# Ranks of the list scheduler: a table in the source instead of a search at build time

## The chip, the cores and the metric

The kernel runs on one core of a Trainium2 chip. The metric is the device time of one execution in microseconds (us), median of three runs. TensorE (PE) multiplies, its weight loads (PEld) run beside it, VectorE (DVE), ScalarE (ACT) and GpSimd (POOL) work on tiles, and SyncE (SP) issues the DMAs. Each engine works through its own instruction list strictly in order and waits on semaphores of the others.

## The reference

Attention with capped scores, then two mixing blocks, all in 32-bit floats:

```python
scores = scale * np.matmul(q, k.transpose(0, 1, 3, 2))
scores = cap * np.tanh(scores / cap)
attn = np.exp(scores - np.max(scores, axis=-1, keepdims=True))
attn = attn / (np.sum(attn, axis=-1, keepdims=True) + 1e-09)
x = np.matmul(attn, v)                      # 4 batches, 12 heads, 448 rows, 64 wide
theta = x @ w_theta                         # x now 4 x 448 x 768
y = einsum(w_tok_r, x * cos(theta)) + einsum(w_tok_i, x * sin(theta))
u = x + y
x = u + np.maximum(u @ w_ch, 0.0)
h = np.maximum(x.T @ w_tok1, 0.0) @ w_tok2  # along the sequence, 256 wide
u = x + h.T
out = u + np.maximum(u @ w_ch1, 0.0) @ w_ch2  # 1536 wide
```

## The kernel before

The program is written as a recording: each call on an engine goes to `Plan.rec`, which makes an `Op` with its engine, its duration by a formula (`cost`), a rank (`prio`, the number of the call plus offsets such as -100 for weight loads) and its dependencies. At the end `Plan.emit` asks `Plan.plan` for an order of all 3872 Ops and writes the instructions out in that order; so every instruction of the trace has line L473.

`schedule` is a list scheduler: it keeps a clock, and whenever an engine is free it takes the ready Op of lowest rank, provided the rotating buffers that it needs (`SB`, `PS`: three `raw` tiles, two double PSUM tiles `pa`, four single ones `pm` and so on) are free and next in turn. Buffers of one tag are handed out in the order in which they were recorded. What was promised a buffer and can't have it goes to a list `waiting`, and comes back when one of that tag comes free. `schedule` also knows some habits of the chip as rules: a table load on ACT costs 1.3, a change of PE's tile form costs up to 0.19, a DMA lands 1.6 after its turn on one common queue plus `LATE`, and a DVE instruction whose operands all lie in SBUF takes up to 0.9 of its own duration longer while POOL is at work.

`plan` runs `schedule` 30 times; after each, `hurry` looks at PE's waits and lowers the rank of what came late. From the best of these `settle` tries 300 random changes of a few ranks near a wait and keeps those that don't lengthen the planned span.

What is computed, in the order of the recording: attention (`attn`) batch by batch in pairs of heads: scores into `pa` (named `sp`), tanh and exp on ACT (`t`, `tm`), products with V (`av`), row sums (`sm`, or in `av` for batches 2 and 3), then `finish`: DVE copies the product (`XT` or `xr`) and the sums (`sv`) out of PSUM, a DMA brings the sums into `pk`, DVE adds and inverts them, a DMA writes them to DRAM (`sr`), another brings them back spread over the partitions (`dn`), and DVE multiplies. For batch 0 `close` does this with two matmuls (`sel`, `spread`) instead. Beside attention the weights are converted (`convert`: a raw 64-bit tile `raw` becomes `cw`, then a high and a low part; DVE, ACT and POOL share the steps, and the result goes to DRAM and comes back as `w`, `WT`, `W`). Woven into batches 1 to 3 are the two mixing blocks of batches 0 and 1: `th` (theta), `rc` (its sine and cosine, on ACT and DVE), `tp` (transposes of `rc`), `zn` (their split into two parts), `tm` (mixing along the sequence), `wc`, `xp`/`xn`/`t`/`h` (the second block along the sequence), `c` (the wide products). PE has its last matmuls of attention shortly before 400 us; from 410 us on it runs the wide products of these two batches, and from 585 us on both mixing blocks of the other two.

The lines that matter for the change: the constants of the search (L80 to L86), `plan` with its helpers (L265 to L323), and the two places in `schedule` that take waiting Ops back (in `allocatable` and where a buffer comes free).

Of the kernel before, what the change touches and what calls it, by code (L numbers as in the profile page):

```python
# [5 lines left out]

# [158 lines left out]
class Plan:  # L165
# [111 lines left out]
    def settle(self, out):
        rng = random.Random(7)
        span, gaps, starts = self.span, self.gaps(out), [o.start for o in out]
        for _ in range(TRIES):  # L280
            at = rng.choices([g[0] for g in gaps], [g[1] for g in gaps])[0]
            near = [o for o in self.ops if at - 14.0 < o.start < at + 1.0]
            some = rng.sample(near, min(len(near), rng.choice((1, 2, 4, 8))))
            old = [(o, o.prio) for o in some]
            for o in some:
                o.prio += rng.uniform(-30.0, 12.0)
            new = self.schedule()
            if self.span < span + 1e-6:
                span, out, gaps = self.span, new, self.gaps(new)
            else:  # L290
                for o, x in old:
                    o.prio = x
                for o, x in zip(out, starts):
                    o.start = x
            starts = [o.start for o in out]
# [2 lines left out]
    def gaps(self, out):
        end, found = 0.0, []
        for o in out:  # L300
            if o.eng == "PE":
                if o.start - end > 0.05:
                    found.append((o.start, o.start - end))
                end = max(end, o.start + o.dur)
        return found

    def hurry(self, out):
        ops, end, late = self.ops, 0.0, set()
        for o in out:
            if o.eng != "PE":  # L310
                continue
            if o.start - end > 0.3 and o.deps:
                x, n = o, 0
                while x.deps and n < HOPS:
                    d = max((ops[i] for i in x.deps), key=lambda y: y.wait)
                    if d.wait < end - 12.0:
                        break
                    if d.start > d.ready + 0.2:
                        late.add(d.n)
                    x, n = d, n + 1  # L320
            end = max(end, o.start + o.dur)
        for n in late:
            ops[n].prio -= PUSH  # L323
# [1290 lines left out]
```

## Time and profile before

| | |
|---|---|
| median of 3 runs | 939.85 us (937.0 to 941.76) |
| the profiled execution | 940.55 us |
| its span, first to last instruction | 938.8 us |
| granted TensorE clock, mean | 0.996 |
| PE busy | 916.3 us |
| PEld busy | 715.5 us |
| DVE, ACT, POOL busy | 614.9, 464.5, 286.5 us |
| instructions | 13346 |

The profile is of one execution. A busy time is the union of an engine's instructions; a wait of PE shorter than the tail of the matmul before it doesn't show as idle. "Idle before" with an engine behind an arrow names what ended the wait. PEclk is the share of full TensorE speed that was granted. The names of tiles are the program's, without buffer numbers. The profiled execution is 0.7 us longer than the median, and 1.75 us longer than its own span.

### The profile page before, as it was taken

How to read it: one execution, taken by the hardware profiler on the slowest of the kernel's cores; microseconds unless marked ns; L12 is line 12 of the kernel's file. 1: busy time of each engine (PE TensorE's matmuls, PEld its weight loads, DVE VectorE, ACT ScalarE, POOL GpSimd, SP SyncE). 2: the span in 40 equal slices, each digit the busy share in tenths (PEclk: the TensorE clock that was granted, in tenths of full speed). 3: DMA queues.
4: the chain of work that ended last, by engine and by line, in shares of the span. 5: the costliest groups of instructions: out<-in, count | busy, mean ns of one | idle time of the engine just before them, and what ended most of it. 6: DMA issues, size and time to landing. Idle time of an engine off the chain costs nothing.

```text
span 938.8 us, 13346 instructions
## 1 busy us (share of the span) xinstructions
PE 916.3 (98%) x4875; PEld 715.5 (76%) x4875; DVE 614.9 (65%) x1022; ACT 464.5 (49%) x743; POOL 286.5 (31%) x231
## 2 busy tenths in 40 slices
PE   8898999999999989999999999999999999999998
PEld 2222665656666667789999999999899999999997
DVE  7997879787795565756656584444794678445342
ACT  6787887977975646524354360424531254021010
POOL 3554334352243222103223261111641264311000
PEclk9999999999999999999999999999999999999999
DMA  6777756575547853246868769811213114443232
GB/s 211 258 251 259 227 170 210 186 265 171 174 126 229 277 150 116 88 138 215 279 206 259 224 225 296 319 35 68 84 40 132 48 55 123 128 159 100 90 127 92
DMA packets 80090, 159.80 MB, mean 170 GB/s; under 512 B 10264, under 2 KB 60312, under 8 KB 80024
## 3 DMA queue, kind: packets, MB, share of 16 engines
q1 hardware_dynamic: 80024, 158.95, 52.6%
q8 instruction: 38, 0.62, 0.3%
q14 instruction: 28, 0.23, 0.1%
HBM read 111.61 MB, written 47.18 MB: 169 GB/s over the span
## 4 chain that ended last, share of the span: by engine, by line
PE 78%; ACT 4%; DMA 3%; DVE 3%; POOL 1%; issue 1%; SPq 0%; ACTq 0%; POOLq 0%
PE c L473 29%; PE P L473 10%; PE th L473 8%; PE tm L473 7%; PE t L473 7%; PE wc L473 6%; PE av L473 5%; PE sp L473 3%; PE tp L473 2%; PE xp L473 1%; DMA raw<-wu 1%; ACT t L473 1%; DMA pk<-sv 1%; DMA dn<-sr 1%; POOL cw L473 1%
## 5 line engine op out<-in xcount | busy, mean ns | idle before, releaser
L473 PE MATMUL c<-g,w 128*128 128x448 f32 x816 | 166.6, 364 | 0.0
L473 POOL TENSOR_TENSOR cw<-cw,raw 128x384 uint32<-128x384 uint32 (+2 forms) x94 | 97.8, 1042 | 219.9 <-DVE cw L473 172.4
L473 PEld LDWEIGHTS c<-g,w 128*128 128x128 f32 x816 | 153.0, 187 | 12.1
L473 PE MATMUL tm<-WT,zn 128*128 128x448 f32 x483 | 108.2, 372 | 0.0
L473 PE MATMUL c<-XHL,w 128*128 128x448 f32 x522 | 107.8, 366 | 0.0
L473 PEld LDWEIGHTS c<-XHL,w 128*128 128x128 f32 x522 | 97.8, 188 | 8.7
L473 PEld LDWEIGHTS tm<-WT,zn 128*128 128x128 f32 x483 | 88.3, 188 | 13.2 <-ACT zn L473 2.1
L473 PE MATMUL th<-XHL,w 128*128 128x448 f32 x432 | 97.6, 372 | 0.0
L473 DVE TENSOR_TENSOR XT<-c,XT 128x448 f32<-128x448 f32 x68 | 42.3, 623 | 80.3 <-PE c L473 80.2
L473 PEld LDWEIGHTS th<-XHL,w 128*128 128x128 f32 x432 | 79.1, 188 | 14.3 <-issue 5.9
L473 ACT ACTIVATE t<-sp,consts 128x896 f32<-128x896 f32 x72 | 72.2, 1004 | 30.1 <-PE av L473 10.9
L473 ACT ACTIVATE t<-t,consts 128x896 f32<-128x896 f32 x72 | 74.8, 1044 | 1.8
L473 POOL TENSOR_TENSOR t<-t,t 128x896 f32<-128x896 f32 x24 | 53.4, 2227 | 64.7 <-PE av L473 30.6
L473 POOL TENSOR_TENSOR XHL<-XT,XHL 128x448 fp32r<-128x448 f32 x36 | 47.8, 1338 | 74.9 <-ACT XHL L473 49.3
L473 PE MATMUL av<-t,vt 128*64 128x448 f32 x288 | 66.5, 565 | 3.1 <-ACT t L473 2.9
L473 PE MATMUL wc<-XHL,w 128*128 128x448 f32 x306 | 67.1, 373 | 0.0
L473 DVE SCALAR_TENSOR_TENSOR cw<-raw,cw 128x384 uint32<-128x384 uint32 (+2 forms) x94 | 64.7, 688 | 2.5
L473 PEld LDWEIGHTS wc<-XHL,w 128*128 128x128 f32 x306 | 57.2, 190 | 11.8 <-issue 7.0
L473 ACT CAST w<-cw 128x384 fp32r<-128x384 f32 x72 | 34.6, 508 | 36.2 <-PE c L473 17.7
L473 DVE TENSOR_TENSOR w<-cw,w 128x384 fp32r<-128x384 f32 x72 | 49.6, 706 | 3.3 <-ACT w L473 2.6
L473 PE MATMUL sp<-kq 64*128 64x448 f32 (+1 forms) x240 | 47.2, 576 | 2.8 <-ACT t L473 2.7
L473 PEld LDWEIGHTS av<-t,vt 128*64 128x64 f32 x288 | 16.3, 137 | 41.8 <-issue 20.7
(171 smaller groups left out, 1453.6 us busy)
## 6 DMA issues: line engine op xcount, KB each, us to landing
w<-cu SPq DMA_DIRECT2D x47, 768.0 KB
raw<-wu SPq DMA_DIRECT2D x72, 384.0 KB
cu<-w SPq DMA_DIRECT2D x72, 384.0 KB
kq<-kqd SPq DMA_DIRECT2D x24, 448.0 KB
vt<-vd SPq DMA_DIRECT2D x24, 224.0 KB
f<-cw SPq DMA_DIRECT2D x28, 192.0 KB
F<-f SPq DMA_DIRECT2D x28, 192.0 KB
out<-XT SPq DMA_DIRECT2D x24, 224.0 KB
```

The lines of the kernel that those rows point to most:

```text
L473: getattr(eng[o.eng], name)(*map(real, a), **{x: real(y) for x, y in k.items()})
```

## The change

The search at build time (`settle`, `gaps`, `hurry` and the loop in `plan`) is taken out. Instead a string of 77 lines holds 3872 whole numbers, compressed; Op number n gets the rank n + 0.5 times its number, which takes the place of the recorded rank with its offsets too. `schedule` then runs once. The numbers were worked out beforehand by a longer search of the same kind. In `schedule` itself one thing is different: when a buffer comes free, only those waiting Ops come back that hold the next buffer in turn (`wake`), where before all that waited for the tag came back to be tried again.

```diff
-ROUNDS = 30
-TRIES = 300
-HOPS = 6
-PUSH = 15.0
+RANKS = r"""
+c-kG92V9or_r`BPG-vK|{M1UV{#t38X64F}WontLVOmydWtlTantLxaH<`E>BBkQM#TErIL>z!1h)9Tn!27<>^PKblzI^xq56^qw=RW7Ut}|}Tyu#=qF?V
...
+"""
     def plan(self):
-        best = None
-        first = {o.n: o.prio for o in self.ops}
-        for _ in range(ROUNDS):
-            out = self.schedule()
-            if best is None or self.span < best[0]:
-                best = self.span, {o.n: o.prio for o in self.ops}
-            self.hurry(out)
-        for o in self.ops:
-            o.prio = best[1][o.n]
-        return self.settle(self.schedule())
...
+        shift = np.frombuffer(zlib.decompress(base64.b85decode("".join(RANKS.split()))), "<i2")
+        for o, x in zip(self.ops, shift, strict=True):
+            o.prio = o.n + 0.5 * x
         return self.schedule()
...
-                for n in waiting.pop(tag, ()):
-                    heapq.heappush(ready[ops[n].eng], (ops[n].prio, n))
+                wake(tag)
             return None
+
+        def wake(tag):
+            want = self.order[tag][nxt[tag]] if nxt[tag] < len(self.order[tag]) else None
+            some = [n for n in waiting.get(tag, ()) if any(b is want for b in ops[n].bufs)]
+            for n in some:
+                waiting[tag].remove(n)
+                heapq.heappush(ready[ops[n].eng], (ops[n].prio, n))
...
-                        for n in waiting.pop(b.tag, ()):
-                            heapq.heappush(ready[ops[n].eng], (ops[n].prio, n))
+                        wake(b.tag)
```

The 3872 Ops, their dependencies and the buffers are the same in both programs; the number of instructions differs only in waits and in ACT's table loads (22 before, 20 now). Within their engine's list half of PE's Ops move by two places or more, the furthest by 28. A change of tile form comes 325 times on PE before and 320 times now. The order at three places:

**PE and DVE in batch 1, where `finish` waits for its DMA (135 to 145 us of the trace).** DVE, before: the sums of one head are inverted (`RECIPROCAL pk`), and four rows later another product is multiplied by its `dn`.

```order
L473 SCALAR_TENSOR_TENSOR pk_1189<-pk_1189,consts 56x16
L473 RECIPROCAL pk_1189<-pk_1189 56x16
L473 TENSOR_TENSOR zn_1283<-tp_1264,zn_1277 128x384
L473 TENSOR_SCALAR cw_1319<-cw_1319 128x384
L473 SCALAR_TENSOR_TENSOR cw_1319<-raw_1151,cw_1319 128x384
L473 TENSOR_TENSOR XT<-XT,dn_1280 128x448
L473 CAST XHL<-XT 128x448
```

DVE, now:

```order
L500 SCALAR_TENSOR_TENSOR pk_1187<-pk_1187,consts 56x16
L500 RECIPROCAL pk_1187<-pk_1187 56x16
L500 TENSOR_SCALAR cw_1310<-cw_1310 128x384
L500 SCALAR_TENSOR_TENSOR cw_1310<-raw_1216,cw_1310 128x384
L500 TENSOR_TENSOR XT<-XT,dn_1239 128x448
L500 CAST XHL<-XT 128x448
L500 TENSOR_TENSOR XT<-tm_1101,XT 128x448
```

Now the multiplication that stands there is that of the head before, whose `dn` is issued on SP ahead of the `pk` load that the first row needs; before, SP issued that `dn` behind it. The head that stood there before is multiplied 13 rows further down, behind the transposes shown next. PE, before (two groups of transposes of one `rc`):

```order
L473 MATMUL th_1315<-XHL,w_953 128x448 x6
L473 MATMUL tp_1372<-ident,rc_1110 128x128 x4
L473 MATMUL sp_1380<-kq_975 128x448 x2
L473 MATMUL tp_1396<-ident,rc_1110 128x128 x3
L473 MATMUL av_1239<-tm_1254,vt_992 64x448
L473 MATMUL av_1404<-tm_1254,vt_1174 64x448
```

PE, now:

```order
L500 MATMUL th_1334<-XHL,w_940 128x448 x3
L500 MATMUL tp_1355<-ident,rc_1107 128x128 x4
L500 MATMUL th_1334<-XHL,w_940 128x448 x12
L500 MATMUL tp_1385<-ident,rc_1107 128x128 x3
L500 MATMUL av_1184<-tm_1236,vt_963 64x448
L500 MATMUL av_1394<-tm_1236,vt_1110 64x448
```

Between the two groups of transposes stood two score matmuls, and now stand twelve matmuls of theta.

**DVE in batch 3, where a product leaves PSUM (340 to 350 us).** `COPY xr` empties the PSUM tile that PE's next scores (`sp`) need; `cw` are steps of `convert`. Before:

```order
L473 SCALAR_TENSOR_TENSOR h_551_3252<-t_550_3192,h_551_3252 128x512
L473 COPY sv_3290<-av_3046 128x448
L473 TENSOR_TENSOR XT<-t_559_3263,XT 128x448
L473 TENSOR_SCALAR cw_3248<-cw_3248 128x384
L473 SCALAR_TENSOR_TENSOR cw_3248<-raw_3134,cw_3248 128x384
L473 COPY xr_3305<-av_3046 128x448
L473 TENSOR_TENSOR XT<-t_560_3279,XT 128x448
```

DVE, now:

```order
L500 TENSOR_TENSOR w_3216<-cw_2887,w_3216 128x384
L500 TENSOR_TENSOR xn_3244<-xp_3219,xn_3232 112x4x128
L500 TENSOR_TENSOR xn_3244<-xp_3210,xn_3232 112x4x128
L500 TENSOR_SCALAR cw_3242<-cw_3242 128x384
L500 COPY xr_3263<-av_3063 128x448
L500 SCALAR_TENSOR_TENSOR cw_3242<-raw_2925,cw_3242 128x384
L500 TENSOR_TENSOR t_3098<-t_3098,t_3164 128x896
```

Before, the copy stood four rows behind that of the sums and behind two steps of `convert`. Now it stands 13 rows behind that of the sums, but PE has moved the other way: between the last `av` matmul that writes this tile and the scores that need it there were a pair of `av`, three `t` and three `wc` matmuls, and now there are six `av`, 24 `t` of 256 columns and 12 `t` of 448 columns.

**DVE in the mixing of batches 2 and 3 (615 to 620 us).** `zn` is read by PE's next `tm` group; `rc<-th` are the first two steps on a new theta. Before:

```order
L473 TENSOR_TENSOR rc_5642<-rc_5642,XT 128x448
L473 TENSOR_TENSOR XT<-tm_5570,XT 128x448
L473 TENSOR_TENSOR XT<-tm_5596,XT 128x448
L473 TENSOR_TENSOR zn_5687<-tp_5614,zn_5622 128x512
L473 TENSOR_SCALAR rc_5699<-th_5648 128x448
L473 SCALAR_TENSOR_TENSOR rc_5699<-th_5648,rc_5699 128x448
L473 TENSOR_TENSOR zn_5687<-tm_5596,zn_5622 128x384
```

DVE, now:

```order
L500 TENSOR_TENSOR zn_5571<-th_5487,zn_5557 128x384
L500 TENSOR_TENSOR rc_5619<-rc_5619,XT 128x448
L500 TENSOR_SCALAR rc_5681<-th_5641 128x448
L500 TENSOR_TENSOR XT<-tm_5565,XT 128x448
L500 TENSOR_TENSOR XT<-tm_5581,XT 128x448
L500 SCALAR_TENSOR_TENSOR rc_5681<-th_5641,rc_5681 128x448
L500 TENSOR_TENSOR zn_5701<-tp_5614,zn_5624 128x512
L500 TENSOR_TENSOR zn_5701<-tm_5581,zn_5624 128x384
```

The first row of the two `rc<-th` now stands ahead of two additions to `XT`, the second directly ahead of `zn`; before, `zn` came first. On PE six `tm` matmuls and ten transposes stand between the theta matmuls that these rows need and the `tm` group that needs `zn`.

Elsewhere, in the attention of batch 1 (80 to 90 us), PE had three `av` pairs in a row, the sums, and then three score groups in a row; now `av` and `sp` alternate.

## Rows read from the trace of the kernel before

**Rows 1.** The page: busy time by engine, and one costly group.

```profile
PE 916.3 (98%) x4875; PEld 715.5 (76%) x4875; DVE 614.9 (65%) x1022; ACT 464.5 (49%) x743; POOL 286.5 (31%) x231
...
L473 POOL TENSOR_TENSOR t<-t,t 128x896 f32<-128x896 f32 x24 | 53.4, 2227 | 64.7 <-PE av L473 30.6
```

**Rows 2.** Busy time by stretch; columns in its first line, clock and DMA as shares.

```profile
core 0: us, PE busy (x) PEld busy (x) DVE busy (x) ACT busy (x) POOL busy (x), PEclk, DMA share, GB/s
0.00:78.00 78.00, 71.66 (x386) 19.79 (x390) 70.30 (x137) 57.84 (x69) 38.85 (x33) 1.00 0.76 256
78.00:92.00 14.00, 11.14 (x64) 3.04 (x58) 9.29 (x19) 10.15 (x13) 5.21 (x5) 1.00 0.57 174
...
125.00:150.00 25.00, 23.05 (x119) 13.31 (x118) 19.79 (x35) 19.50 (x32) 9.26 (x7) 0.93 0.70 217
...
275.00:300.00 25.00, 23.37 (x124) 16.99 (x123) 18.52 (x38) 14.85 (x30) 10.23 (x9) 1.00 0.72 211
...
343.00:353.00 10.00, 7.63 (x33) 4.44 (x30) 6.62 (x8) 2.96 (x4) 3.11 (x2) 0.83 0.57 150
...
399.00:404.00 5.00, 4.44 (x31) 3.75 (x30) 2.98 (x5) 2.02 (x3) 0.00 (x0) 1.00 0.56 130
...
680.00:938.80 258.80, 255.22 (x1340) 236.18 (x1338) 143.24 (x212) 58.81 (x112) 59.57 (x50) 1.00 0.31 99
```

**Rows 3.** Timeline of PE, 78 to 92 us: start, us, work, idle before.

```profile
80.98 0.97 PE L473 MATMUL av<-t,vt 128*64 128x448 f32 x4 [0.56 <-ACT t L473]
82.95 0.97 PE L473 MATMUL av<-t,vt 128*64 128x448 f32 x4 [1.00 <-ACT t L473]
...
89.58 1.94 PE L473 MATMUL sp<-kq 64*64 64x448 f32 x12 [0.95 <-ACT t L473]
```

**Rows 4.** The chain that ended last, 125 to 149 us: start, us, what.

```profile
131.77 7.28 DMA dn<-sr
...
144.00 0.90 PE tp L473 x3
```

**Rows 5.** Busy time by stretch behind two waits; clock is the third number from the end.

```profile
144.00:146.00 2.00, 2.00 (x11) 0.81 (x11) 1.97 (x4) 1.09 (x3) 0.00 (x0) 0.50 1.02 357
146.00:148.00 2.00, 2.00 (x12) 0.45 (x12) 1.54 (x5) 1.95 (x4) 0.00 (x0) 0.67 0.94 317
...
349.00:351.00 2.00, 2.00 (x6) 0.58 (x3) 0.94 (x2) 0.44 (x1) 0.00 (x0) 0.50 0.76 113
351.00:353.00 2.00, 2.00 (x9) 1.80 (x8) 0.00 (x0) 1.97 (x3) 0.00 (x0) 0.72 0.78 299
```

**Rows 6.** Timeline of all engines, 342 to 351 us.

```profile
344.31 2.10 POOL L473 TENSOR_TENSOR t<-t,t 128x896 f32<-128x896 f32 x1 [1.85 <-PE av L473]
344.35 2.28 DVE L473 TENSOR_SCALAR cw<-cw 128x384 uint32<-128x384 uint32 x1
...
347.14 0.62 DVE L473 COPY xr<-av 128x448 f32<-128x448 f32 x1
...
347.90 0.86 PE L473 MATMUL sp<-hl 64*128 64x448 f32 x6 [2.37 <-DVE xr L473]
```

**Rows 7.** Timeline of DVE, 615 to 620 us.

```profile
617.49 0.68 DVE L473 TENSOR_TENSOR zn<-tp,zn 128x512 fp32r<-128x512 f32 x1
618.17 0.62 DVE L473 TENSOR_SCALAR rc<-th 128x448 int32<-128x448 f32 x1
```

**Rows 8.** Timeline of PE in the same stretch.

```profile
615.52 1.38 PE L473 MATMUL tm<-WT,zn 128*128 128x448 f32 x6
...
618.30 0.60 PE L473 MATMUL tp<-ident,rc 128*128 128x128 f32 x4
618.65 1.68 PE L473 MATMUL tm<-WT,zn 128*128 128x448 f32 x7
```

**Rows 9.** Timeline of DVE, 408 to 421 us.

```profile
409.89 0.24 DVE L473 RECIPROCAL pk<-pk 56x16 f32<-56x16 f32 x1
...
420.15 0.63 DVE L473 TENSOR_TENSOR xr<-xr,dn 128x448 f32<-128x448 f32 x1 [1.70 <-DMA dn<-sr]
```

More of the change, by code (lines that the diff above doesn't have):

```diff
@@ L1 @@
+import base64
 import heapq
-import random
 import math
 import re
+import zlib
 from contextlib import ExitStack, contextmanager
@@ L92 @@
 PAT2 = (1, 0, 0, 1, 0, 0, 0)
+RANKS = r"""
+c-kG92V9or_r`BPG-vK|{M1UV{#t38X64F}WontLVOmydWtlTantLxaH<`E>BBkQM#TErIL>z!1h)9Tn!27<>^PKblzI^xq56^qw=RW7Ut}|}Tyu#=qF?V
+B*Uk;0Fc=_^`=(z9y?UkH)G4T5Q)Io^@qFN=4xwJC2_~N3JUv5@UZhN~^@``KIVykDBTu#5)`cAi)?MXdz)ANI3{bD|hEIGUGe$>7ESV=hjZ-
+<<_53akub+5PQII(s$^I7VU|AMnC$S|vmw6-
+#>;dUq4=@{P$7uLD!c<Pt6^AuVU&N`prxsK0n`BD1W>zvsdVIOif%L4Z&a!mG>z30yJv7Fx}P&dkR5`pEI%B!q3vc;L;_LY3uC%;=G?1S=HE9()R;G{TjN
+|rOxPVzgchjplKbhgPy=CIYpd2*wde?y%kr7~NRt4)-
+Z@|_HHp4g9_9rg@QCDT;`<TH(RW?8H4D^`kq(lg1VSd*+D@M)9%oHW&QI#!oSZwa(#d!p=i);pd$PDSgw-NonLHTA4g;~C=2^eneiJQ<$(POfLR&+nQlSI
@@ new lines @@
+kgtEJN%J_bq#*9cQnx=UJVcPzfoiUtHV%Rc6T{Yl7X*DY75gW%fuX)3wIA;_-
+EooM}#!oobJfxt^AC&*|aBdivI!;uLx|y6W1e?8o+BmEW~TOILe}{e=~6f37{MSMk)aXW9Ao{>K$6k8`%#U9A7<eUEW{@0woYzGs-
+z+J45gc$n%Ob7tCMl5L-I{H%kn8Lk++zms7Fm-
+ct6+HLz3m1VfQSlddRvNok7%i8KD=c=7#b+uaA{VHs7HMNFWfu&OF?>T0@ZwGi1tOVQF`QBOV+;;bM=UQLM30dkcbTzhqk;bl-rA5V)CBJNGNlDQwPkwkZ
+P-d5Y?&|)?%-iYlSOuQ7PKB~J-
+BoRuYkFCjXNFeLF8YIt=MDE!tD#fJ`qQ=2J<49_X>HfBJ6Qca8?1As<4XHlN8BG;bv^YwStXN8p0>A?Y$$%NB(SW1NonbUJ+~iiay!;==ZL23TJ5Nz`ixn
+vr^_N;9bE5QuX<K%h)mKUI!EgmV@l;a-CEMi<y%(ha;#X_q_WOg#qK6gW|w{A=_O&BA-_tL4AJkf6d^10mX5^YWOd9Nra;WR0e1Y80_zRWOOh?~^=&gsYn
@@ new lines @@
+s}o^V^r*8j&u4$-X14gE^7_e-KF-qG!uO8p@vXm{}@YoaJq=Iv(euZbTpIadnkE3-ujsT;HLy#RUw*-REOU*gH_A%qK>|VRx-
+7c*~Uo=h$)7@c7Q_)Ip(c=+o%U6dO~ZOO6DWD&1C=IDESrB8EdDhp84$bGq>?E5>6lLLi~F`1w4nndH9%sHnwRbiaG)sizH7ivN#2+xA4Q)Jk2Tj*x74sA
+>$rto})0k0Z(_4UqR(Dtp<Z5WNfikHM#s=q_2T$h9;q@*N7{MD5E*;4q0^yJP+#*Im6CD+MFnI&~Of1CBx53VvE-
+H<`UUE4^JY=!4+s_m!1Uq)8OlCzBEC+bAh;zse+2b^$(DAQ0O`Q3ucO_iPA0**HKV>pWP2M&PkJ($)i>pCZjcr49N$PN#w~e?LgMd;p|G}L=eoUYAf?6HR
+*4C8!R`VhY0Pa4RskfZp5F8rir-
+*Lq%YB87~7lJ5#%&v)}M{15x!wQHG5BL<{6Ctk1@yC=hB&9FgS4b8zl&{v`w4`Z@0csD%fpk2%r{+%k2BY{j#o#C#W39@TorTLZGlvxemSCf>C*?aXP;_(
@@ new lines @@
+<-8Bl=2anGDhzDEL#}MH5|fQ=iW-$$I|UhL7J<NgA*+hDmJ%YDtvcME5y2=@gJX3!@2~vmJXgs077S-WW7;iRmnam_tD!7aN<gnFUw*Al;4Z-
+l?yn&HCuzH>yKV6!kIKdi8vb$<vo!a-N)CkG&7ze<v87#g_M;(S$0wlxXXjfby)l4;SmSqj?K_g3)vc(Rg5g8Q$cOw<lo#C<q<o=NN2mqt=Zg-
+>aF~Sbl(~NANrZn=`53t++jSSM4A-3(4MOvg$as-
+f+LWi!U`yEz^m)^D($~fM3IG_9FiN&C^(Xf68p2mbD=>EKYg_Mk_EKEkV7z@wqMjKSX)guy~dHkAThDoS&uM3YP?~^;usA3WMoR1GF)>jl+0;njPufEUI$
+1-
+a#$h3nFJ=;)ygNFW<p(7+?3P6bD%Uy!nmDikKL^chf8^W^%?CXw+a&m>(?e(%U(|GTeND`fAHu&O8Oi+wda}`_tu9ZUS?ino@)NQnbus$0D@$BdYNBlSuu
@@ new lines @@
+C{G86-rFgmtZ1<qqsd7u|$v}NyrlaI!Ch90SZ_MvW?CMA)Mc%um{H%?nBlBK&vTF$_jAQy8r+-
+Sj@|#Tr6OoI!4in{U{T9!<ps5$|_@P*we+l%$VIxZ}q3DiaGmg`4$tTiGduV_4!}C3G|B^W@8FEVMn#uIn=4OB{HQS{g*!HKE%$GcOknLDu)(Ldh7=4a(#
+xuvf3I8*s6rB2NkW<Zm;)!>EX&rKM?P@Ysrb<m>zTxFYQ=~|4N(&8>Z28$t)!oh<n93pU!#V^nJJVmUz(fhv`Bk&VFu8GyZvaOVVY4!~{av6vge<Q?1@qn
+zl2F(v)0j`*VGg~f{mcTe4M!FI`MZ{R-3&%;--
+2`j87{C|s)OjtS#X*S2j2hc?B{6{6I3!MHD%hGr^983^pWP$z<8%(?|tP<{7mHYr<h4DP)m2<^Ad8T2K6+TzPy6GtWSSzNe&#L6FnfJt-
+OgRTa(F_id5F?)X_QcdmEMgp>w1*Sig<3(qxyMrso|1r{nln&3wwuJ)HUBYB?(LSo;?(UxL%t#(Pt_tzKU}<x|1$%r?<v#WzfZk>DK0&wXfgKJOpmV-io*
@@ new lines @@
+$@&0J-N0>WJXPM9-DGPHmUEd?9-
++i|wCufMU6Xz~h@2aNo_<AnYk5v*df=`iy@|+}_ULmQ_xIso(}0@sF|{EOKTGH)dtmQl*cp%3;=w!^&oat+Nny|XRJDQFNTd@?m3VnqE5KR<>P0J13kM%&
+b<-b@4SC#!-K$}(2DKuYK2`^fHv!cp=zThwyBKe;a!;sBl-
+~aV2B5<$U>YN>^eN4huGm{b#W_WnDj*A|P;<|qp{w9`k9*i2n7K)n8OC=b^9OY(p6C*_r>Si6;d?E0_ZEA5qK7`5_AYVVA$Rv-
+>nQ$QFaIxSHYe0$%E%|WpWyF3ko$soH)&JU;hj~!;uBx9g4#We>i@F&1T_t3-
+9_xI;f(WS;)nF7&0uka>8lDH&j8aO==O6oUJj^34{B>hi1&ZSbG0RYPr<t+PD`e{d8fhwu(<*>Lzz8JX^t$G9^4%6OQ9Ttp~0wg3L1zfeivQl1GuSTwvvw
+t@)NzKfOFs0hS~;io4|U8__3=1Ej<Cj4e-
@@ L95, in regroup @@
+5QBW0qv<d~#NOKQbJ*^2)MsQ+icq&hR%Id2}q#|r!&uilF5&u7<V7E$J6bshTY2M&X%XCq+j1bWWa8{&_@U!&QfRIDX>TpF=!CjE9S@h#VX#ak2qL)&-
+ob0_RG&oJLzE>}?~evL*Amr?i`>Zf;Np9&sVz{4<)gyQ*rGHt!yl`*iBL!CZS&i*aba)DiIVd6DB-a)Q(<@-
+20Ccwsxa;^0v&*ITZqUK2eI`GcG{ZQR<?0ipF1o2lb{IsMk(S8n(G3<^Z|FW3_6ZHQ9X5!<8
+"""
 def regroup(shape, pattern, sizes):
@@ L265, in plan @@
     def plan(self):
-        best = None
-        first = {o.n: o.prio for o in self.ops}
-        for _ in range(ROUNDS):
-            out = self.schedule()
-            if best is None or self.span < best[0]:
-                best = self.span, {o.n: o.prio for o in self.ops}
-            self.hurry(out)
-        for o in self.ops:
-            o.prio = best[1][o.n]
-        return self.settle(self.schedule())
[L277 to L295, printed above, removed]
-        return self.schedule()
@@ L298, in gaps @@
[L298 to L323, printed above, removed]
+        shift = np.frombuffer(zlib.decompress(base64.b85decode("".join(RANKS.split()))), "<i2")
```

36 lines of the change are left out of this document (added).

## The prediction

> **What bounds the kernel now.** I read the page first: PE is busy 916.3 of 938.8 us of span [rows 1], so its waits that show make 22.5 us, and no reordering can give back more than these and what the clock loses behind them. Then I asked where they lie, with the table of stretches [rows 2]: 6.34 us in the first 78 us (78 less 71.66), 2.86 from 78 to 92, 1.95 from 125 to 150, 1.63 from 275 to 300, 2.37 from 343 to 353, 0.56 from 399 to 404, and 3.58 behind 680 us, most of it the tail after the last matmul, which no rank can shorten. What these stretches leave of the 22.5 us, 3.2, is spread out. The clock column adds a loss that isn't idle time: 0.93 over 25 us is 1.75 us, 0.83 over 10 us is 1.7 us. So the floor for any order is near 940.55 - (22.5 - 3.6) - 3.45 = 918.2 us, and the question is how much of 22 us the table gets. Behind 404 us PE waits little; the change is decided in the first 404 us, and there by single places.
>
> **The change, part by part.** Work: nothing is added or removed, since the Ops are the same; the changes of tile form on PE are 325 before and 320 now, and two table loads less on ACT lie beside PE's work. I cost both at nothing. The `wake` rule brings back the one Op that can get its buffer instead of all; those others would have gone back to the list, so it costs nothing either, unless a form or table preference chose among them. What is left are places.
>
> *Attention, 0 to 92 us.* Before, PE did three `av` pairs in a row and waited for ACT's exponentials ahead of the second and third, 0.56 and 1.00 us, and then three score groups in a row, with 0.95 us ahead of the next [rows 3]. Now `av` and `sp` alternate, so ACT gets scores while PE does products. ACT was busy 10.15 us of these 14 and PE 11.14 [rows 2]; fully overlapped, 11.1 would do. Since two steps of ACT follow each other for each score group, I take 2.0 of the 2.86 us as gone (bounds 0 and 2.86). In the first 78 us ACT is at work 57.84 us and DVE 70.30, the order on PE is much the same, and part of the 6.34 us is the first load. I take 1.5 (bounds -1 and 3).
>
> *125 to 150 us.* The chain of waits shows DVE held by a DMA, `dn<-sr`, for 7.28 us until 139.05, a row of late DVE work behind it, and PE's transposes at 144.00 at the end [rows 4]. PE idles 1.95 us, and then runs at a granted clock of 0.50 from 144 to 146 and 0.67 from 146 to 148, that is at the lower of its two levels, 1.2 GHz, for more than 3 us [rows 5]; this loses 2 x 0.50 + 2 x 0.33 = 1.66 us. The place costs 3.6 us. Now the multiplication that stood there has its DMA wait 13 rows later, the one in its place has a DMA that SP issues before one that DVE needs anyway, and PE has twelve theta matmuls between the two transposes instead of two score matmuls. I take all 3.6 as gone (bounds 0 and 3.6).
>
> *275 to 300 us.* Of 1.63 us, one score group more ahead of the product that waited takes 0.86, the length of such a group at 347.90 [rows 6]: 0.8 (bounds 0 and 1.6).
>
> *343 to 353 us.* DVE's copy of `xr` comes at 347.14, behind a step of `convert` that took 2.28 us beside an addition of POOL of 2.10; PE waits 2.37 us for it [rows 6], and then has a clock of 0.50 and 0.72 in the two stretches from 349 to 353 [rows 5], a loss of 2 x 0.50 + 2 x 0.28 = 1.56. Together 3.9 us. Now some 40 matmuls stand between the last product in that tile and the scores that reuse it, instead of eight. All 3.9 gone (bounds 0 and 3.9).
>
> *399 to 404 us.* Between transposes and the matmuls that read them stood one group; now there are three small groups and one of sums. 0.5 of 0.56.
>
> Gone: 2.0 + 1.5 + 3.6 + 0.8 + 3.9 + 0.5 = 12.3 us.
>
> *Added, near 616 us.* `zn` now stands behind both `rc<-th` steps and two additions. From the end of theta: four DVE steps of about 0.62 and `zn` with 0.68 [rows 7], 3.2 us, and 0.2 for the handing over. PE has meanwhile six `tm` matmuls, at most 1.38, and ten transposes, at 0.09 each by the 0.35 us from the start of four to the next group [rows 8], together 2.2 us. PE waits some 1.2 us where it didn't (bounds 0 and 1.6); I take 1.3, with the transposes' own wait for `rc`.
>
> *Places that I can't see.* Two of the largest waits before came of what the planner doesn't know: the DMA took 7.28 us, and the step of `convert` is booked with 0.16 + 0.00052 x 384 = 0.36 us and at most 0.9 times that on top, 0.68, but took 2.28. The new order was fitted to the same planner and will meet such things at other places. The price of a place where they reach PE is 3.6 to 3.9; the old order had two in full. I take one, 3.8 us (bounds none and three, 0 to 11.4), since the slack at the known places has grown.
>
> A rule of the skill bears on this. The row shows that the DVE step ended at 346.63, just after POOL's addition at 346.41 [rows 6]. The Trainium skill says, in "SBUF — State Buffer", section "SBUF: two separate sides", that VectorE and GpSimd share one pair of ports as an exclusive lock, and that the loser blocks for the whole instruction; the row agrees. By this rule each of POOL's 24 additions of that shape, 2227 ns on average [rows 1], can hold a DVE step up to 1.6 us longer than the planner thinks, in either order alike, and the closer the table follows the planner, the less it leaves for that. This speaks against the change, and is the reason for the second case below, whose time comes from the rows.
>
> **Sum.** 12.3 gone less 1.3 and 3.8 leaves 7.2 us: 940.55 - 7.2 = 933.35 for an execution like the profiled one, which lies 0.7 above the median; so 932.6, rounded **932.5 us**.
>
> **The rivals.** A measurement can tell about 0.5% here, 4.7 us: faster is under 935.2, slower over 944.5.
>
> *No new place.* All of 12.3 is kept but for the 1.3: 940.55 - 11.0 - 0.7 = 928.9. For it: every known place has more PE work in front of it than before, and two of the larger waits weren't the order's fault alone. Against it: DVE is busy 70.30 of the first 78 us [rows 2], with little room for a lock.
>
> *Planned away, not gained.* The table is better only by the planner's account: two or three new places at 3.8 us stand where two went, and the time is 936.4 to 940.2. For it: the two mechanisms that cost most are outside of the planner. Against it: the clock fell behind a single long wait at both places, and PE's list now has more between producer and user at each of them.
>
> *Slower.* DVE stands at a `dn` multiplication for its DMA, and all behind it on DVE comes late, among it copies that free PSUM. The shortest way that the trace shows, with DVE waiting at its end, is from the inversion at 409.89 + 0.24 to the multiplication at 420.15, 10.0 us, of which DVE waited 1.70 [rows 9]. Where an order leaves DVE less than 10 us of work between the two, DVE waits; In the new order some of these stretches of DVE work are shorter than before, more are longer. Each costs up to the 3.6 of the place at 144 us; this decides against the change from the fourth new place on: with five, 940.55 - 11.0 + 19 - 0.7 = 947.9.
>
> **How the numbers follow.** One new place, 932.5: 0.36. None, 928.9: 0.27. Two or three: 0.26. Four or more: 0.11. Faster than 935.2 are the first two and a small part of the third (0.03), where the places cost less than in full: 0.66. Slower than 944.5 is most of the last: 0.10. The rest, 0.24, is the same. The range: the known places at the far ends of their bounds (2.86 + 3 + 3.6 + 1.6 + 3.9 + 0.56 = 15.5), with nothing added, give 940.55 - 15.5 - 0.7 = 924.3, and 0.8 of the 3.2 us of spread waits 923.5; above, three new places and 2.3 for places that keep half of their wait give 942.5.
>
> **What would show it.** In the changed kernel: PE's idle time under 15 us in sum; no stretch with a clock under 0.9 near 125 to 150 and 343 to 353 us; PE's waits for ACT `t` cut from 78 to 92 us; a wait for DVE `zn` or `rc` of about 1.3 us near 610 us. I am wrong if the clock falls at two or more new places, if DVE's waits for `dn<-sr` grow, or if the first 78 us hold more than 7 us of waits.

## The result, and the profile after

The changed kernel takes 927.14 us (median of 4 runs, 926.38 to 928.48) where the kernel before, run beside it, took 939.6 (937.0 to 941.76). The ratio is 0.987, with a 95% interval of 0.984 to 0.990. It is faster, and the time lies in the range, 5.4 us under the predicted 932.5. The profiled execution took 927.71 us against 940.55, which is 12.84 less.

The page of the changed kernel, busy time by engine, answers to [rows 1]:

```profile
PE 914.0 (99%) x4875; PEld 714.4 (77%) x4875; DVE 601.2 (65%) x1022; ACT 462.1 (50%) x741; POOL 282.1 (30%) x231
```

PE's idle time is 926.0 less 914.0, 12.0 us; it was 22.5. Where it went, the table of stretches of the changed kernel shows, which answers to [rows 2] (length, busy time of PE, PEld, DVE, ACT and POOL, granted clock, DMA share, GB/s):

```profile
0.00:78.00 78.00, 73.15 (x398) 20.21 (x398) 70.74 (x139) 59.03 (x70) 39.10 (x34) 1.00 0.75 243
78.00:92.00 14.00, 13.04 (x58) 4.09 (x59) 5.88 (x18) 12.44 (x15) 5.57 (x5) 0.88 0.76 239
125.00:150.00 25.00, 25.00 (x132) 17.30 (x132) 21.57 (x35) 19.98 (x34) 10.10 (x8) 1.00 0.74 227
...
275.00:300.00 25.00, 25.00 (x132) 16.41 (x131) 17.04 (x30) 14.06 (x24) 9.04 (x9) 1.00 0.75 233
...
343.00:353.00 10.00, 10.00 (x64) 6.17 (x64) 5.62 (x10) 7.48 (x11) 1.57 (x2) 1.00 0.15 54
...
399.00:404.00 5.00, 5.00 (x26) 4.58 (x25) 1.47 (x3) 0.52 (x1) 0.00 (x0) 1.00 0.02 4
...
680.00:926.00 246.00, 242.38 (x1273) 224.37 (x1272) 135.86 (x203) 56.14 (x106) 56.88 (x47) 1.00 0.31 102
```

From 125 to 150, 275 to 300, 343 to 353 and 399 to 404 us PE never stands, at full clock. One place is new, and the clock column gives it away: 0.88 from 78 to 92 us, where it was 1.00. PE's timeline there (start, us, work, idle before):

```profile
72.16 1.02 PE L500 MATMUL sp<-kq 64*128 64x448 f32 x4
...
75.66 0.97 PE L500 MATMUL av<-t,vt 128*64 128x448 f32 x4
78.62 1.02 PE L500 MATMUL sp<-kq 64*128 64x448 f32 x4 [2.00 <-ACT t L500]
```

ACT's timeline over the same time, and POOL's step that ACT waited for:

```profile
71.69 1.04 ACT L500 ACTIVATE t<-t,consts 128x896 f32<-128x896 f32 x1
77.28 0.38 ACT L500 CAST WT<-cw 128x224 fp32r<-128x224 f32 x1 [4.55 <-POOL cw L500]
77.57 1.00 ACT L500 ACTIVATE t<-sp,consts 128x896 f32<-128x896 f32 x1
```

```profile
76.59 0.66 POOL L500 TENSOR_TENSOR cw<-cw,raw 128x224 uint32<-128x224 uint32 x1 [1.00 <-issue]
```

This is the picture to learn. The scores that the tanh at 77.57 reads were written well before, from 72.16 us on, but ahead of it in ACT's list stands a step of `convert`, a CAST that waits 4.55 us for GpSimd. ACT can't pass it, the tanh starts late, and PE, which needs the tanh's PSUM tile back for its next scores, stands 2.00 us. Then the clock falls, as the stretches of 2 us show:

```profile
78.00:80.00 2.00, 1.32 (x6) 0.50 (x8) 1.92 (x8) 1.97 (x3) 0.28 (x1) 1.00 0.99 358
80.00:82.00 2.00, 2.00 (x8) 0.51 (x4) 0.08 (x1) 1.90 (x4) 2.00 (x2) 0.53 0.90 321
82.00:84.00 2.00, 2.00 (x8) 0.29 (x4) 0.98 (x2) 1.97 (x2) 0.54 (x1) 0.62 0.05 18
```

That loses 2 x 0.47 + 2 x 0.38 = 1.7 us more. Two smaller waits, at 179.90 (1.28) and 190.01 us (1.07), have the same cause: a step of `convert` on ACT, waiting for GpSimd (the first) or for a transfer (the second), ahead of a ready tanh.

### The profile page after: what moved, and what is told of

It is laid out like the page before. It is cut to its first block, busy times and chain, and to the rows that moved or that the text cites. A ratio compares the mean times of both kernels' runs of the same rounds, so it can differ in the third digit from the quotient of the medians.

```text
span 926.0 us, 13338 instructions
## 1 busy us (share of the span) xinstructions
PE 914.0 (99%) x4875; PEld 714.4 (77%) x4875; DVE 601.2 (65%) x1022; ACT 462.1 (50%) x741; POOL 282.1 (30%) x231
## 4 chain that ended last, share of the span: by engine, by line
PE 82%; DVE 9%; DMA 5%; issue 1%; ACT 1%; SPq 1%; POOL 0%; POOLq 0%; DVEq 0%
PE c L500 30%; PE P L500 10%; PE th L500 9%; PE tm L500 8%; PE wc L500 7%; PE t L500 7%; PE av L500 5%; PE sp L500 4%; DVE cw L500 4%; DMA pk<-sv 2%; PE tp L500 2%; DMA raw<-wu 2%; PE xp L500 1%; DVE XT L500 1%; DMA dn<-sr 1%; DVE sv L500 1%
## 5 line engine op out<-in xcount | busy, mean ns | idle before, releaser
L500 PE MATMUL c<-g,w 128*128 128x448 f32 x816 | 169.4, 364 | 0.0
L500 PEld LDWEIGHTS c<-g,w 128*128 128x128 f32 x816 | 153.0, 187 | 12.1
L500 PE MATMUL tm<-WT,zn 128*128 128x448 f32 x483 | 110.1, 373 | 0.0
L500 DVE SCALAR_TENSOR_TENSOR cw<-raw,cw 128x384 uint32<-128x384 uint32 (+2 forms) x94 | 75.0, 799 | 2.4
L500 POOL TENSOR_TENSOR XHL<-XT,XHL 128x448 fp32r<-128x448 f32 x36 | 44.3, 1240 | 73.5 <-ACT XHL L500 46.6
L500 DVE TENSOR_TENSOR w<-cw,w 128x384 fp32r<-128x384 f32 x72 | 44.9, 642 | 9.2 <-ACT w L500 9.2
```

The costliest lines, as they stand in the source:

```text
L500: getattr(eng[o.eng], name)(*map(real, a), **{x: real(y) for x, y in k.items()})
```

## The experiments

The first four runs keep one of the two orders and move single operations in it (the numbers are their places in the program's order of recording). The edit stands in `emit`, and k is 0 for "ahead of m", 1 for "behind m":

```
         order = self.plan()
+        for n, m, k in MOVES:
+            o = next(x for x in order if x.n == n)
+            order.remove(o)
+            order.insert(next(i for i, x in enumerate(order) if x.n == m) + k, o)
```

### e1: the copy ahead of the convert steps, in the kernel before

```
+MOVES = ((1540, 1831, 0),)
```

> The kernel before, with one instruction moved: on VectorE the copy of the accumulator into the tile xr (1540 in the plan), which TensorE's score product at 347.90 us waited for, stands ahead of two convert steps (1831, 1832) instead of behind them. Theory, that each place is worth its wait and what the clock lost behind it: 2.37 us of wait and 1.56 us of clock go, 3.9 us, so about 935.7 against 939.6 (ratio 0.996), and the granted clock between 349 and 353 us reads 1.00 where it read 0.50 and 0.72. Rival, that the wait only passes on to the next late operand: under 1 us gained, and a new wait of TensorE over 1.5 us within the 20 us behind. A half-way result, 2.4 us, would mean that the clock falls there without the wait too.

Measured: 935.85 us, ratio 0.995 (0.994 to 0.997). DVE's and PE's timelines of this run, and the stretches behind (they answer to [rows 5, 6]):

```profile
344.06 0.61 DVE L480 COPY xr<-av 128x448 f32<-128x448 f32 x1
344.60 1.77 DVE L480 TENSOR_SCALAR cw<-cw 128x384 uint32<-128x384 uint32 x1
```

```profile
345.18 0.88 PE L480 MATMUL sp<-hl 64*128 64x448 f32 x6
```

```profile
349.00:351.00 2.00, 2.00 (x12) 1.83 (x11) 1.43 (x4) 0.16 (x1) 0.00 (x0) 1.00 0.80 164
351.00:353.00 2.00, 2.00 (x17) 0.72 (x15) 0.27 (x2) 0.57 (x1) 0.00 (x0) 1.00 0.71 256
```

The copy no longer stands behind the long convert step, the scores follow with no wait, and the clock stays at 1.00. The gain is 3.4 us in the median, for 3.9 expected; by the interval it is 2.8 to 5.7. So one moved instruction brought about as much as the two terms of this place said. Part of the agreement is chance, though: in the profile of e1 the clock doesn't fall behind the wait at 144 us either (2.06 us there), where nothing was changed; the last section comes back to this.

### e2: the multiply behind the ready instructions, in the kernel before

```
+MOVES = ((534, 685, 1), (535, 534, 1), (536, 535, 1))
```

> The kernel before, with three instructions moved: on VectorE the multiply by dn (534, and 535 that follows from it), which stood waiting for its transfer at the head of the queue from 137.4 to 139.1 us, goes behind the five ready instructions that stood behind it (645, 642, 646, 660, 685); GpSimd's third step of the same split (536) goes behind the convert step 710. Theory of single places: TensorE's transpose at 144.00 no longer waits 1.95 us, and the clock of 0.50 and 0.67 between 144 and 148 us does not fall, 1.66 us: together 3.6 us, about 936.0 (ratio 0.996). Rival, that the wait passes on: under 1 us.

Measured: 941.44 us, ratio 1.002 (1.001 to 1.004): slower by 2.2 us, where 3.6 less was expected. The transposes' wait went, and a new one came 17 us later. The SP queue, DVE, ACT and PE in turn:

```profile
142.87 0.54 SPq L480 DMA_DIRECT2D dn<-sr  x1
```

```profile
151.27 0.62 DVE L480 TENSOR_TENSOR XT<-XT,dn 128x448 f32<-128x448 f32 x1 [3.48 <-DMA dn<-sr]
...
156.34 0.61 DVE L480 TENSOR_TENSOR XT<-tm,XT 128x448 f32<-128x448 f32 x1
```

```profile
157.04 0.57 ACT L480 CAST XHL<-XT 128x448 fp32r<-128x448 f32 x1 [4.50 <-DVE XT L480]
...
159.71 1.02 ACT L480 ACTIVATE t<-sp,consts 128x896 f32<-128x896 f32 x1
```

```profile
160.78 0.87 PE L480 MATMUL sp<-hl 64*128 64x448 f32 x6 [2.22 <-ACT t L480]
162.87 3.79 PE L480 MATMUL tm<-WT,zn 128*128 128x448 f32 x10 [0.41 <-DVE zn L480]
```

The moved multiply is what frees the only buffer of `dn`. The next transfer into it was issued 3.15 us later than before, the next multiply stood 3.48 us for it, DVE's row behind came late, a CAST on ACT waited for that row with a tanh some steps behind it, and PE waited for the tanh. From 163 to 167 us the clock is 0.57 and 0.58. The rival is right here, in a form that I hadn't written down: the wait passed on through a buffer.

### e3: three places at once, in the kernel before

```
+MOVES = ((1540, 1831, 0), (534, 685, 1), (535, 534, 1), (536, 535, 1),
+         (424, 427, 1), (437, 440, 1), (451, 454, 1))
```

> The kernel before with the moves of the last two runs, and at 79 to 90 us TensorE's three score products taken from behind the three value products and set between them (value, score, value, score, value, score, sum). Theory, places add up: 3.9 and 3.6 as above and 2.5 for the three waits for ScalarE (0.56, 1.00, 0.95): 10.0 us, 929.6 (ratio 0.989), most of what the changed kernel gained (12.5 us) by ten moved instructions out of nearly four thousand. Rival, that a gain at one place is lost at the next and only the whole table gives the time: under 5 us.

Measured: 939.96 us, ratio 1.001 (0.999 to 1.002): nothing gained. The copy's place is mended as in e1, the multiply's loses as in e2, and the attention passes its waits on. ACT and PE in this run:

```profile
86.32 0.38 ACT L480 CAST WT<-cw 128x224 fp32r<-128x224 f32 x1 [3.08 <-POOL cw L480]
86.60 1.00 ACT L480 ACTIVATE t<-sp,consts 128x896 f32<-128x896 f32 x1
```

```profile
87.66 1.02 PE L480 MATMUL sp<-kq 64*128 64x448 f32 x4 [3.45 <-ACT t L480]
```

Three waits of 2.5 us in sum went, and one of 3.45 came, behind the same kind of CAST; the clock fell after it. So the places don't add up, and the gain of the table isn't that of a handful of moved operations (seven here).

### e4: tanh ahead of the waiting convert steps, in the changed kernel

```
+MOVES = ((394, 318, 0), (395, 318, 0), (398, 318, 0), (399, 318, 0),
+         (299, 234, 0), (852, 943, 0), (1126, 889, 1), (1125, 1126, 1))
```

> The changed kernel, with ScalarE's order mended at its four longest waits of TensorE: at 60, 77, 178 and 188 us a convert step that waits (for GpSimd, at 188 us for a transfer) stands ahead of a tanh whose scores are ready; the tanh goes ahead of it. Theory, that these new places are each a blocked head of ScalarE's queue: waits of 0.55, 2.00, 1.28 and 1.14 us and 1.7 us of clock (0.53 and 0.62 between 80 and 84 us) go: 6.7 us, about 920.5 against 927.1 for the changed kernel, ratio 0.980 to the kernel before. Rival, that VectorE and GpSimd, which convert the weights late, are the limit there: the waits move to the products behind, and under 2.5 us is gained (over 924.6).

Measured: 925.57 us, ratio 0.985 (0.984 to 0.987), 1.6 us under the changed kernel where 6.7 was expected, and the two intervals overlap. The waits at 60, 179 and 190 us are gone or under 0.2 us; that at 78.62 moved to 85.25, behind the next CAST that waits for GpSimd, and the clock fell there (0.54 and 0.60 from 86 to 90 us):

```profile
83.92 0.38 ACT L507 CAST WT<-cw 128x224 fp32r<-128x224 f32 x1 [1.69 <-POOL cw L507]
84.20 1.00 ACT L507 ACTIVATE t<-sp,consts 128x896 f32<-128x896 f32 x1
```

```profile
85.25 1.02 PE L507 MATMUL sp<-kq 64*128 64x448 f32 x4 [1.89 <-ACT t L507]
```

The time is the rival's (over 924.6 us). By the rows theory and rival share this one: three places were a blocked head of ACT's queue and no more; at the fourth, ACT's converting is late altogether.

### e5: the old release rule with the table

```
-                wake(tag)
+                for n in waiting.pop(tag, ()):
+                    heapq.heappush(ready[ops[n].eng], (ops[n].prio, n))
```

(and the same where an operation's buffers come free).

> The changed kernel with its table, but with the release rule of the kernel before in the scheduler (a freed buffer puts every waiting operation back into the ready lists, not only the one whose turn it is). The order differs in 11 of TensorE's operations, 4 of ScalarE's, 2 of VectorE's and 4 of GpSimd's. Theory, that the time comes from the table: within 1 us of the changed kernel, 926.1 to 928.1 (ratio to before 0.986 to 0.988). Rival, that the rule carries part of the gain: over 929.1.

Measured: 927.61 us, ratio 0.988 (0.986 to 0.989). The rule is worth nothing that shows; the time comes from the table. This run has the same wait as the changed kernel, and yet the clock didn't fall behind it:

```profile
78.83 1.02 PE L502 MATMUL sp<-kq 64*128 64x448 f32 x4 [1.85 <-ACT t L502]
```

```profile
80.00:82.00 2.00, 1.96 (x10) 0.53 (x12) 0.20 (x2) 1.97 (x3) 2.00 (x1) 1.00 0.97 349
```

### e6, e7 and e10: the same search, longer

Here the order is read whole from a table, and the table comes from the search of the kernel before, with the new release rule and the planner's own costs, after 3000 and 40,000 tries. Against the changed kernel (`...` marks lines left out):

```
     def plan(self):
-        shift = np.frombuffer(zlib.decompress(base64.b85decode("".join(RANKS.split()))), "<i2")
...
-        return self.schedule()
+        order = np.frombuffer(zlib.decompress(base64.b85decode("".join(ORDER.split()))), "<i2")
+        self.span = float(SPAN)
+        return [self.ops[i] for i in order]
```

> A dose of the search: the order that the search of the kernel before finds with 3000 tries in place of 300, with the planner's costs as they are. The planner's own idea of the span is 932.5 us; it was 938.0 for the kernel before (939.6 measured) and 927.5 for the changed one (927.1 measured). Theory, that what the planner takes out of TensorE's gaps is gained on the chip, with an offset between -0.4 and +1.6 us: 932.1 to 934.1, ratio 0.993. Rival, that a new order meets as many new waits by chance as it loses planned ones: over 936 (ratio over 0.996).

> The same search with 40,000 tries, from another seed than any run so far and with nothing taken from the changed kernel's table: the planner's own idea is 927.8 us, next to the 927.5 of the changed kernel's table. Theory, that length of search is all there is in the table: 927.4 to 929.4, ratio 0.988. Rival, that the table holds something that the planner's measure does not show (an order picked by its time on the chip, say): over 931 (ratio over 0.991).

> The planner's own costs again, 40,000 tries from the first seed; the planner's idea is 928.4 us. The run with 927.8 took 932.1, the changed kernel's table with 927.5 took 927.1. Theory, that orders of equal plan scatter on the chip by the waits that the planner does not see: anywhere from 926 to 934, and TensorE waits longest at other places than in either. Rival, that the changed kernel's table is of a kind of its own: 931 to 934 again.

| order | planner's idea, us | measured, us | ratio (interval) | measured less planned | PE's idle time in the profile, us |
|---|---|---|---|---|---|
| before, 300 tries | 938.0 | 939.6 | 1 | +1.6 | 22.5 |
| e6, 3000 tries | 932.5 | 936.62 | 0.997 (0.996 to 0.998) | +4.1 | 20.9 |
| e7, 40,000 tries | 927.8 | 932.07 | 0.992 (0.991 to 0.994) | +4.3 | 18.4 |
| e10, 40,000 tries, other seed | 928.4 | 934.49 | 0.995 (0.993 to 0.997) | +6.1 | 19.0 |
| the changed kernel's table | 927.5 | 927.14 | 0.987 (0.984 to 0.990) | -0.4 | 12.0 |

All three missed what was expected of them, on the slow side (e10 by half a microsecond against its own wide range); the numbers of e6 and e7 are those of their rivals (over 936 and over 931). A longer search does make the kernel faster: against the runs of before that stood beside them, e6, e7 and e10 gain 2.3, 6.8 and 5.0 us of the 5.5, 10.2 and 9.6 that they plan. The rest goes to waits that the planner doesn't see: e7 and e10 have some 6 to 7 us more idle time of PE than the changed kernel, at plans that differ by less than 1 us. In e6 the clock has a share as well: its one run at a mean granted clock of 0.999 took 932.2 us, the others, at 0.993 to 0.998, took 935.1 to 939.1. In e10, ACT and PE once more:

```profile
78.85 0.38 ACT L479 CAST WT<-cw 128x224 fp32r<-128x224 f32 x1 [3.04 <-POOL cw L479]
```

```profile
83.09 3.26 PE L479 MATMUL av<-t,vt 128*64 128x448 f32 x8 [3.84 <-ACT t L479]
```

In e6 the longest wait is 3.50 us at 299.34, for DVE's copy `sv`. The changed kernel's table stands 5 and 7 us better than two orders of nearly the same plan. Whether it is a lucky one among many, or was picked by a measure that knows the chip, these runs don't tell.

### e8 and e9: other costs in the search

> The same instructions in an order searched with other costs: durations of each kind of instruction as the traces of the runs so far show them, a VectorE instruction without a PSUM operand held until GpSimd's instruction is nearly done, and each candidate order played through five times with transfers up to 0.8 us and GpSimd's steps up to 0.1 us later, in place of the planner's fixed costs. By the planner's own costs this order is bad, 934.8 us (before 937.9, changed 927.5). Theory, that the 12 us in which TensorE still stands in the changed kernel are places that the planner mis-costs: most of those outside the first 78 us and the end (3.2 us of 12) go, and part of the 4.85 us of the first 78, so 919 to 924, taken 921.5 (ratio 0.980). Rival, that the planner's measure is the better one: about 935.

> As the last, from another seed, whose order is played through 3 us longer (921.8 against 918.7 with fresh delays; by the planner's own costs 937.9). Theory: 3 us behind the last, 922 to 927, taken 924.5. Rival, the planner's measure: about 938.

The edit is that of e6, with another table. Measured: e8 927.12 us, ratio 0.987 (0.984 to 0.989), no better than the changed kernel and 5.6 us behind what was taken; e9 924.31, ratio 0.984 (0.982 to 0.986), as taken. By the planner's costs both should be 7 to 10 us slower than the changed kernel (934.8 and 937.9 for 927.5), so its measure is refuted as a judge at this level. The new measure isn't a good one either: it had e9 3 us behind e8 (921.8 and 918.7), and e9 came out 2.8 us ahead, so its hit is in part luck. Which part of the new measure helps, the durations, VectorE held behind GpSimd or the late transfers played through, no run separates. In e9 the attention stretch has neither wait nor fall:

```profile
78.00:92.00 14.00, 14.00 (x71) 5.36 (x70) 12.54 (x23) 12.58 (x17) 8.12 (x7) 1.00 0.73 234
```

e9 is the fastest order found; it beats both kernels in the median, though its interval still overlaps that of the changed kernel.

### e11 and e12: a second buffer for the transfer

```
-            return sb.tile([P, *free], dt, name=n, tag=tag, bufs=SB[tag])
+            return sb.tile([P, *free], dt, name=n, tag=tag, bufs=2 if tag == "dn" else SB[tag])
```

> Run e2 (the multiply by dn moved behind five instructions) with two buffers of dn in place of one, the order of all instructions unchanged. In e2 the next transfer into dn could only be issued at 142.87 us, when the moved multiply had freed the one buffer, 3.15 us later than before, and the next multiply stood 3.48 us for it at 151.27, with ScalarE and at the end TensorE (2.22 us at 160.78, and the clock) behind it. Theory, that this buffer is what turned the gain of e2 into a loss: with two, the transfer is issued some 5 us earlier, the wait at 151 us goes, TensorE's wait at 160.8 falls under 0.5 us, and the gain of 3.6 us shows: 935.6 (ratio 0.996). Rival, that ScalarE is late there for another reason: the wait at 160 us stays over 1.5 us, about 940.

> The control of the last run: the kernel before, its order unchanged, with two buffers of dn. The transfer whose multiply held VectorE until 139.07 us was itself issued when the one buffer came free (131.4 us). Theory: it is issued some 2 us earlier, the multiply does not stand, VectorE's row behind it is 1.6 us earlier, TensorE's wait at 144.00 falls to some 0.3 us and the clock behind it stays: 3.3 us, about 936.0 (ratio 0.9965). Rival, that the transfer waits for its source, not for the buffer: no change, within 1 us of before.

Measured, e11: 937.26 us, ratio 0.998 (0.996 to 0.9995), 4.2 under e2 (3.7 when each is taken against the runs of before beside it). The SP queue and DVE:

```profile
137.76 0.54 SPq L480 DMA_DIRECT2D dn<-sr  x1
```

```profile
147.60 0.62 DVE L480 TENSOR_TENSOR XT<-XT,dn 128x448 f32<-128x448 f32 x1
```

The transfer is issued 5.1 us earlier, the multiply doesn't stand, and PE has no wait for ACT near 160 us. So the buffer was what turned e2's gain into a loss. Of the gain, 1.4 us shows against the kernel before, for 3.6 expected; by the interval it is 0.5 to 3.8. That is about the wait alone: PE's idle time from 120 to 180 us is 0.88 us where it was 2.55. The clock's part doesn't show in the median.

e12: 938.4 us, ratio 0.999 (0.997 to 1.0003), no change, as the rival had it. The SP queue, DVE and PE:

```profile
131.87 0.54 SPq L473 DMA_DIRECT2D dn<-sr  x1
```

```profile
138.74 0.63 DVE L473 TENSOR_TENSOR XT<-XT,dn 128x448 f32<-128x448 f32 x1 [1.14 <-DMA dn<-sr]
```

```profile
143.70 0.55 PE L473 MATMUL tp<-ident,rc 128*128 128x128 f32 x3 [1.23 <-DVE XT L473]
```

In the order of before, this transfer doesn't wait for its buffer: it goes out at 131.87 us with two and at 131.77 with one [rows 4]. In the chain of this run the DMA that writes its source, `sr<-pk`, stands directly ahead of it, 4.96 us until 131.85.

## Why the prediction was right, and where it was off

The forecast was faster, by 7.2 us between the profiled executions; it became 12.84. By its own steps:

- *125 to 150 and 343 to 353 us*, 3.6 and 3.9 forecast: all gone, 1.95 and 2.37 us of idle time and the clock behind them. The reason given for the second, more PE work between the tile's last product and its reuse, shows in the timelines: DVE's copy ends at 332.92 us (the row below) and the scores that need it start at 338.88, where before it ended 0.14 us ahead of them [rows 6]. The reason for the first was half of it: e2 shows that moving the multiply behind its neighbours loses by itself; the table moved everything behind it as well. And the prediction's 7.28 us are the transfer's time, not DVE's: DVE stood 1.63 us for it, at 139.07.

```profile
332.30 0.62 DVE L500 COPY xr<-av 128x448 f32<-128x448 f32 x1
```

- *Attention*, 2.0 + 1.5 us, and *the place that I couldn't see*, 3.8. The new place came, with its clock, where I hadn't looked: in the attention itself, at 78.62 us, for 2.0 + 1.7 = 3.7 us. That is the price foretold; that it was one place and not two was a guess, and that the clock fell behind it belongs to this execution (e5 has the wait without the fall). The step that was mis-sized is the attention's own gain: PE's idle time in the first 92 us fell from 9.20 to 5.81 us, new wait included, so without it by 5.4, for 3.5 forecast. With the clock's loss, these terms together gave 1.7 us, where I had 0.3 lost.
- *275 to 300 us*: 1.63 gone, all of it, for 0.8.
- *399 to 404 us*: 0.56 gone for 0.5.
- *Near 616 us*, 1.3 added forecast: 0.28 us by the row below, for the additions to `XT`, and none for `rc` or `zn`. DVE's row, from 604.26 to 607.24, took 3.0 us where I had 3.4, and PE's ten transposes took 1.4 us without the wait where I had 0.9.

```profile
606.17 0.55 PE L500 MATMUL tm<-ident,rc 128*128 128x128 f32 x3 [0.28 <-DVE XT L500]
```

- *The spread waits*, 3.2 us that I left alone: at 300 to 343 us and at 676 to 680 some 0.5 us each went, 1.0 in sum. All this makes 12.1 of the 12.84 us. Against it, the waits from 150 to 275 us grew from 2.09 to 2.35; what is left, about 1 us, I can't put to a place. Whether the five fewer changes of tile form, which the prediction costed at nothing, have a part in it, no run shows.

So the forecast of 932.5 was off by small terms that nearly all fell to one side, and the time came out near the case *No new place*, 928.9, though its condition did not hold: that nearness is chance. Of the signs, the idle time under 15 us (12.0) and the clock near 125 to 150 and 343 to 353 us (1.00) came as said, the wait of 1.3 us near 610 us did not; the clock fell at one new place, not at two, and the first 78 us hold 4.85 us of waits, not 7.

The rivals. *Planned away, not gained* (936.4 to 940.2) is false for this table, but true as a mechanism: e6 is such an order, e10 nearly, and e7 lost a third of what it planned. As a guess at what a planner's order of nearly this plan brings, 932.5 was good: e7, e10 and the changed kernel average 931.2. *Slower* through DVE standing for `dn` is false for this table and is what happened in e2, with the buffer as the link. My sign for it was a bad one. DVE's waits for `dn<-sr` did grow in the changed kernel, as its list of waits shows (engine, what waits, for what: us in total, times, longest), from 2.6 and 2.2 us before:

```profile
DVE xr L500 <- DMA dn<-sr: 4.1, 3, 2.1
DVE XT L500 <- DMA dn<-sr: 4.0, 2, 2.1
```

The only wait of PE for DVE that its list has behind 92 us is the 0.28 us above, so no cost of these shows there. A wait on an engine beside the path says nothing by itself; what matters is who is next in that engine's list.

The rule of the Trainium skill that I weighed ("SBUF — State Buffer", section "SBUF: two separate sides", the lock of VectorE and GpSimd) holds here in a narrower form, which the section also has: VectorE takes the shared ports only with two inputs in SBUF or in a two-port mode. In the changed kernel, POOL and then DVE beside it:

```profile
148.00 2.51 POOL L500 TENSOR_TENSOR t<-t,t 128x896 f32<-128x896 f32 x1
```

```profile
148.45 0.61 DVE L500 COPY sv<-sm 128x448 f32<-128x448 f32 x1
148.98 1.95 DVE L500 SCALAR_TENSOR_TENSOR cw<-raw,cw 128x384 uint32<-128x384 uint32 x1
```

The copy out of PSUM takes its usual 0.61 us in the middle of POOL's addition; the convert step, which reads SBUF alone and takes 0.56 us when POOL is still, lasts until 0.42 us after POOL's end. Counted over the whole trace, 27 convert steps of this form start while a POOL step on tiles runs and take 1.42 us on average, the 45 others 0.56; 13 such copies start beside POOL and take 0.62, like the rest. Taken together the new order doesn't meet this more often than the old one: the same instructions keep DVE busy 601.2 us, where it was 614.9. But the planner books at most 0.9 of the step's own length for it; in the row shown 1.39 us came on top of 0.56. The new wait at 78.62 has such a row ahead of it. POOL, and DVE's convert step beside it, which takes 0.27 us at 79.34 with POOL idle:

```profile
74.45 1.14 POOL L500 TENSOR_TENSOR XHL<-XT,XHL 128x448 fp32r<-128x448 f32 x1 [0.33 <-DVE XHL L500]
```

```profile
74.48 1.24 DVE L500 TENSOR_SCALAR cw<-raw 128x224 f32<-128x224 f32 x1
```

With DVE's CAST at 73.48, which took 0.90 us where the one at 72.52 took 0.39, some 1.5 us of DVE's lateness there come from such rows, and POOL's step at 76.59 and the CAST at 77.28 follow from that list. That is how a CAST on ACT, which ends the convert chain, comes late for reasons that the planner doesn't have. That this lock is the chief source of the new waits is argued from such rows, not shown by a run of its own.

## What to carry to other kernels

Where engines take their lists in order, look at each long wait for the instruction that stands at the head of the list that the bound engine waits on: here it was often a late conversion ahead of a ready tanh (the longest waits of the attention in the changed kernel, e3, e4 and e10). Before moving one, look at what it frees: the moved multiply held the only buffer of the next transfer, and the move lost more than it gained. A planner's own time orders candidates coarsely (five orders, from 0.4 us under to 6.1 over the plan), and two orders searched with measured costs were faster than three searched with its own (927.1 and 924.3 us for 932.1 to 936.6). Neither measure told the best beforehand, so time several.

## What the runs showed of the hardware

I had charged the clock behind both long waits in full, from one profiled execution, as if it belonged to the wait. It doesn't always come. The same wait of 2.37 us at 347 to 349 us is followed by a fall in the kernel before [rows 5, 6], and by none in e12:

```profile
347.34 0.86 PE L473 MATMUL sp<-hl 64*128 64x448 f32 x6 [2.37 <-DVE xr L473]
```

```profile
349.00:351.00 2.00, 2.00 (x12) 1.81 (x11) 0.37 (x1) 1.76 (x2) 0.00 (x0) 1.00 0.78 204
```

So with the wait at 144 us (1.95 us in the kernel before, with a fall; 2.06 in e1, without) and that at 79 us (2.00 with in the changed kernel, 1.85 without in e5). Nor is its price fixed: in e11, behind the same 2.37 us, at 344.44 us there, the clock is 0.50 from 344 to 350 us, which costs some 3.2 us, twice as much as in the kernel before; the fall at 299 us in e6 costs as much. In the kernel before the clock is back at 1.00 5 us behind the end of the wait, at 353 us; in e11, as long behind it:

```profile
349.00:350.00 1.00, 1.00 (x5) 0.87 (x4) 0.00 (x0) 1.00 (x2) 0.00 (x0) 0.50 0.08 31
```

The falls go with most of the spread of one and the same program: of the 21 runs of the kernel before that stood beside e1 to e4, the 6 at a mean granted clock of 1.000 took 937.4 us in the median, the 8 at 0.998 took 938.9, the 5 at 0.996 took 941.0, and the 2 at 0.995 took 942.5. So a fall is mostly worth some 1.7 us where it comes, and the profiled execution of before, with two, was not a typical one; the terms of 1.66 and 1.56 us were right for it, and too large for the median.
